# Scores of q from two products a half: agents' leading and residual parts side by side as columns

## The chip, the cores and the metric

The kernel runs on one core of a Trainium2 chip. The metric is the device time of one execution in microseconds; the median of three runs is compared. A profile of one further execution gives the trace.

## The reference

Inputs: q, k and v of 2 x 12480 x 128, agents of 2 x 49 x 128, all float32; w_in (128 x 2048) and w_out (2048 x 128) in float64.

```
def sm(a, b):
    s = scale * (a @ b.transpose(0, 2, 1))
    s = s - s.max(-1, keepdims=True)
    e = exp(s)
    return e / (e.sum(-1, keepdims=True) + 1e-9)
agent_v = sm(agents, k) @ v          # 49 x 128 per batch
x = sm(q, agents) @ agent_v          # 24960 tokens x 128
h = x @ w_in
out = maximum(0.01 * h, h) @ w_out
```

Attention through 49 agents, then two layers with a leaky ReLU on every token.

## The kernel before

**Blocks and steps.** The 24960 tokens go in 52 blocks of 480 (26 of each batch), channels first. A block has eight steps p. A step computes 2 x 128 of the 2048 hidden channels (`mm1`, which takes the attention's weights pT straight to hidden channels through a product of agent_v and w_in, in m_hi and m_lo), evicts them through ReLU as a leading part hi (ScalarE, line 702) and a residue lo (VectorE, line 703), and two steps later (LAG = 2) adds them into the output (`mm2`, line 719). Products run on rounded float32 (F32R), so every operand is split into a leading part and a residue, and each product is the sum of three. The linear part of the leaky ReLU is one more product of pT with l_hi and l_lo (line 729), added at p = 4.

**Halves.** In `mm1`, `mm2` and `q_mm` every product contracts over 64 partitions, the lower half (0 to 63) or the upper (64 to 127), and the two of a pair write different banks, g = 0 and g = 1. In `mm1` the halves hold two groups of hidden channels' weights, because pT has all 49 agents in each half; in `mm2` and `q_mm` they are the two parts of a sum, and somebody has to add the banks up. In `mm2` `o_copy` (ScalarE, line 740, one copy of both banks) and `o_add` (GpSimd) do that; the output tile has one buffer, so the first output product of a block waits for the copy of the block before. Program order is o_copy of block i - 1, then `mm1` of block i's step 2, then the side work of the step, then `mm2` of step 0.

**Slots.** The 49 agents stand in four groups of 32 columns (SLOTS): agents 0 to 24, 25 to 48, 25 to 48, 0 to 24, so that 32 x 32 transpositions on VectorE work on them.

**The chain of q.** For every block a chain of small operations makes pT, spread over the steps ahead of the block by the table `chain`: (-14, q_mm) means 14 steps before the block's first. q_hi (ScalarE) and q_lo (GpSimd) split q; q_mm makes the scores (six products, line 589); q_x (ScalarE, line 596) copies bank 1 and q_add (VectorE, line 602) adds bank 0; q_tr transposes; q_red takes a maximum over the agents of a slot; q_swap (GpSimd, lines 618 and 619) exchanges the halves' maxima; q_mx, q_sub, q_exp, q_sum, q_swap, q_rec, q_norm complete the softmax; p_trans transposes back; p_hi and p_lo split it. In a step the instructions are issued in the order `mm1`, ReLU, side work, `mm2`; each engine takes its own in that order. The bank pair of the scores (tag "x", one buffer) is shared with the key scores, the value sums and the weight products of batch 1.

**Around it.** Batch 0's keys, values, weights and its first chain come ahead of the loop, in an order that a planner makes from listed costs; the chain of block 1 is packed into steps 0 to 6 of block 0 (`early`). Batch 1's key scores run in blocks 0 to 6, its weighted values (`k_av2`) in blocks 9 to 21, its weights in 22 to 24.

```
    chain = (
        (-17, q_hi), (-17, q_lo), (-14, q_mm), (-14, q_x), (-14, q_add), (-13, q_tr),
        (-12, q_red), (-12, q_swap), (-11, q_mx), (-11, q_sub), (-9, q_exp), (-8, q_sum),
        (-8, q_swap), (-7, q_rec), (-7, q_norm), (-6, p_trans), (-4, p_hi), (-4, p_lo),
    )
```

Of the kernel before, what the change touches and what calls it, by code (L numbers as in the profile page):

```python
# [8 lines left out]
F32 = mybir.dt.float32  # L9
F32R = mybir.dt.float32r  # L10
# [3 lines left out]
ALU = mybir.AluOpType  # L14
# [49 lines left out]
def tile_agent_attention_then_leaky_mlp(  # L64
# [33 lines left out]
    NB = G * TP  # L100
# [38 lines left out]
    ps_o = ctx.enter_context(tc.tile_pool(name="ps_o", bufs=1, space=PSUM))  # L139
# [15 lines left out]
    w_out_sb = const.tile([P, NF, C], F32, tag="wm", name="w_out_sb")  # L155
    wo_hi = const.tile([P, NF, C], F32R, name="wo_hi")
    wo_lo = const.tile([P, NF, C], F32R, name="wo_lo")
    ww = const.tile([P, C], F32, name="ww")
    a_sb = const.tile([P, B, NA], F32, name="a_sb")
    a_hi = [const.tile([P, P], F32R, name=f"a_hi{b}") for b in range(B)]  # L160
    a_lo = [const.tile([P, P], F32R, name=f"a_lo{b}") for b in range(B)]
    m_hi = [const.tile([P, DFF], F32R, name="m_hi0"), None]
    m_lo = [const.tile([P, DFF], F32R, name=f"m_lo{b}") for b in range(B)]
    l_hi = [const.tile([P, C], F32R, name=f"l_hi{b}") for b in range(B)]
# [110 lines left out]
    wT = {}  # L275
# [15 lines left out]
    def ww_mm(n):  # L291
        for j in range(4):
            f = 4 * n + j
            nc.tensor.matmul(  # L294
                avw[0][:, 1, :C], lhsT=wT[n][:, j * P:(j + 1) * P], rhs=w_out_sb[:, f, :],
                start=False, stop=(f == NF - 1),
            )

    def ww_end():
        nc.scalar.mul(ww, avw[0][:, 1, :C], SLOPE)  # L300

    def scale(eng, o, x, f=1.0, add=0.0):
        if eng is nc.scalar:
# [6 lines left out]
    def sub(eng, o, x, y):  # L310
        eng.tensor_tensor(out=o, in0=x, in1=y, op=ALU.subtract)  # L311


    SLOTS = (0, 0, A0), (SL, A0, NA - A0), (2 * SL, A0, NA - A0), (3 * SL, 0, A0)

    def prep_a(b):
        a = a_sb[:, b, :]
        a_sl = p1.tile([P, P], F32, tag="avs", name="a_sl")
        nc.gpsimd.memset(a_sl, 0.0)
        for o, x, n in SLOTS:  # L320
            nc.vector.tensor_copy(a_sl[:, o:o + n], a[:, x:x + n])
        for o in (SL, 2 * SL):
            nc.vector.tensor_copy(a_sl[:, o + A0 - 1:o + A0], a[:, A0 - 1:A0])
        nc.vector.tensor_copy(a_hi[b], a_sl)
        sub(nc.vector, a_lo[b], a_sl, a_hi[b].bitcast(F32))
# [99 lines left out]
    av_t, avw = {}, []  # L425
# [21 lines left out]
    def av_zero(b, first):  # L447

        if first:
            av_t[b] = avw[0][:, 0, :C + 2]  # L450
        z = m_lo[1][:TP, :C + 2]
        nc.tensor.matmul(av_t[b], lhsT=z[:, :P], rhs=z, start=first, stop=not first)

# [115 lines left out]
    qs_t, s_t, x_t, r_t2, pT_t = {}, {}, {}, {}, {}  # L569
# [12 lines left out]
    def q_mm(i):  # L582
        b = i // BPB
        hi, lo = qs_t.pop(i)
        ps = aux2()
        for n, (w, x) in enumerate(((a_hi, hi), (a_lo, hi), (a_hi, lo))):
            for g in range(2):
                r = slice(g * HALF, (g + 1) * HALF)
                nc.tensor.matmul(  # L589
                    ps[:, g, :NB], lhsT=w[b][r], rhs=x[r], start=(n == 0), stop=(n == 2)  # L590
                )
        s_t[i] = ps

# [4 lines left out]

    def q_add(i):
        ps, x = s_t[i]  # L600
        s = p1.tile([P, NB], F32, tag="sq", name="sq")
        nc.vector.tensor_tensor(out=s, in0=ps[:, 0, :NB], in1=x, op=ALU.add)
        s_t[i] = s

    def q_tr(i):
# [9 lines left out]

    def q_swap(i):
        r = r_t2[i]
        nc.gpsimd.tensor_copy(r[:HALF, :, 1], r[HALF:, :, 0])  # L618
        nc.gpsimd.tensor_copy(r[HALF:, :, 1], r[:HALF, :, 0])

    def q_mx(i):
        r = r_t2.pop(i)
# [55 lines left out]
    h_t, r_t, o_t = {}, {}, {}  # L678
# [30 lines left out]
    def mm2(i, p):  # L709

        b = i // BPB
        if p == 0:
            o_t[i] = ps_o.tile([P, 2, MC], F32, tag="o", name="o")
        o = o_t[i]
        hi, lo = r_t.pop((i, p))

        def add(w, x, start=False, stop=False):
            for g, r in enumerate(ROWS):
                nc.tensor.matmul(o[:, g, :NB], lhsT=w[r], rhs=x[r], start=start, stop=stop)  # L719

        for g in range(2):
            f = 2 * p + g
            add(wo_hi[:, f, :], hi[:, g], start=(f == 0))
            add(wo_lo[:, f, :], hi[:, g])
        if p == NP // 2:
            t = pT_t[i]
            for w, x, g in ((l_hi, 0, 0), (l_lo, 0, 1), (l_hi, 1, 0)):
                r = ROWS[g]
                nc.tensor.matmul(  # L729
                    o[:, g, :NB], lhsT=w[b][r], rhs=t[r, x], start=False, stop=False  # L730
                )
        for g in range(2):
            f = 2 * p + g
            add(wo_hi[:, f, :], lo[:, g], stop=(f == NF - 1))

    def o_copy(i):
        t = p1.tile([P, 2, NB], F32, tag="oT", name="oT")
        o = o_t.pop(i)
        if i < NBLK - 1:
            nc.scalar.copy(t, o[:, :, :NB])  # L740
            x_t["o"] = t
            return
        h = NB // 2
        for c, eng in ((slice(0, h), nc.sync), (slice(h, NB), nc.scalar)):
            nc.scalar.copy(t[:, 1, c], o[:, 1, c])
            nc.vector.tensor_tensor(out=t[:, 0, c], in0=o[:, 0, c], in1=t[:, 1, c], op=ALU.add)
            eng.dma_start(out=out[:, i * NB + c.start:i * NB + c.stop], in_=t[:, 0, c])

    def o_add(i):
# [7 lines left out]
    def at(step, fn, *a):  # L757
        side.setdefault(step, []).append((fn, a))


    chain = (
        (-17, q_hi), (-17, q_lo), (-14, q_mm), (-14, q_x), (-14, q_add), (-13, q_tr),
        (-12, q_red), (-12, q_swap), (-11, q_mx), (-11, q_sub), (-9, q_exp), (-8, q_sum),
        (-8, q_swap), (-7, q_rec), (-7, q_norm), (-6, p_trans), (-4, p_hi), (-4, p_lo),
    )

    early = (0, 0, 0, 0, 1, 1, 2, 2, 3, 4, 4, 5, 5, 6, 6, 6)
    for i in range(1, NBLK):
        at(NP * i + LAG, o_add, i - 1)
    for r, (_, fn) in zip(early, chain[2:]):  # L770
# [8 lines left out]
    for b in range(1, B):  # L779
# [3 lines left out]
        for c in range(NCH):  # L783
            s = n0 + c // 2 * NP
# [33 lines left out]
        for m in range(0, NM, 2):  # L818
            s = n0 + 5 + (m // 2 + 1) * NP
# [5 lines left out]
    with tc.manual_schedule():  # L825
        nc.sync.dma_start(out=a_sb, in_=agents)
        loads = [(x, ORDER[:i].count(x)) for i, x in enumerate(ORDER)]
        warm = m_lo[1][:, :MC]
# [8 lines left out]
        for t in [pd] + er:  # L837
            nc.gpsimd.memset(t.bitcast(F32), 0.0)

        avw.append(ps_o.tile([P, 2, MC], F32, tag="o", name="avw"))  # L840

        def heat(n, start=False):

            for i in range(n if ("wmm", NM - 1) not in plan.done else 0):
                nc.tensor.matmul(
                    avw[0][:, 1, :], lhsT=warm[:, :P], rhs=warm, start=start and i == 0, stop=False
                )

        plan = Plan(HOP, {"pe": 6000, "dve": 6500, "act": 2500, "pool": 5000, "dma": 3000})
# [12 lines left out]
        dve, act = nc.vector, nc.scalar  # L862
# [24 lines left out]
        for n in range(2 * NM):  # L887
            r = [("mul", n - RP)] if n >= RP else []
            add(("bits", n), "dve", 940, conv_bits, (n,), [("w", n)] + r)
            add(("mant", n), "act", 620, conv_mant, (n, act), [("bits", n)])  # L890
            add(("exp", n), "act", 1440, conv_exp, (n,), [("bits", n)])
            add(("low", n), "dve", 620, conv_low, (n,), [("mant", n)])
            add(("sign", n), "dve", 680, conv_sign, (n,), [("exp", n)])
            add(("mul", n), "dve", 600, conv_mul, (n, dve), [("low", n), ("sign", n)])
            if n % 2:
                add(("wohi", n), "act", 620, wo_hi_of, (n, act), [("mul", n)])
            if n == 1:
                add(("wolo", n), "dve", 680, wo_lo_of, (n,), [("wohi", n)])
# [16 lines left out]
        for c in range(NCH):  # L915
# [91 lines left out]
```

## Time and profile before

| what | value |
|---|---|
| median of 3 runs | 981.24 us (981.02 to 981.54) |
| profiled execution | 980.12 us, its span 978.3 us |
| TensorE busy, mean granted clock | 961.8 us, 1.000 |
| VectorE, ScalarE, GpSimd busy | 727.1, 602.8, 385.6 us |

The span runs from the first to the last instruction; 1.8 us of the profiled execution lie around it. Busy times are shares of the span; TensorE overlaps products, so its busy time says that something was in flight, not how much.

### The profile page before, as it was taken

The page shows a single profiled execution, that of the slowest core. Times are in us where ns is not written, and L with a number is a line of the kernel's source. Part 1 is how long each engine was busy: PE and PEld are TensorE (multiplying, and loading weights), DVE is VectorE, ACT ScalarE, POOL GpSimd, SP SyncE. Part 2 cuts the span into 40 slices and gives each one's busy share as a digit, 9 for nine tenths or more (in the row PEclk, how much of TensorE's full clock was granted, in tenths as well). Part 3 has the DMA queues.
Part 4 walks back from the last instruction along what each step waited for, and adds up shares of the span by engine and source line. Part 5 has one row for each costly group of instructions (what it writes and reads, how often), then busy time and mean ns, then how long its engine had stood idle before and what let it go on. Part 6 is the DMA issues. An engine that isn't in the chain of part 4 may idle for free.

```text
span 978.3 us, 22378 instructions
## 1 busy us (share of the span) xinstructions
PE 961.8 (98%) x9336; PEld 824.4 (84%) x9336; DVE 727.1 (74%) x1071; ACT 602.8 (62%) x806; POOL 385.6 (39%) x557
## 2 busy tenths in 40 slices
PE   8889999999999999999999999999999999999998
PEld 6767888888888888888888888888888888888886
DVE  6967677778787787787776777777777777677764
ACT  5755565566666666665665666665666666666653
POOL 2113233346666556563443333333333333333320
PEclk9999999999999999999999999999999999999999
DMA  9931112112112122110010101101010101010000
GB/s 347 368 139 63 62 62 91 53 42 83 42 42 82 43 59 65 41 42 22 21 41 22 42 21 33 31 22 42 21 42 21 41 21 42 21 37 26 22 21 21
DMA packets 24032, 57.68 MB, mean 59 GB/s; under 512 B 2787, under 2 KB 16355, under 8 KB 23931
## 3 DMA queue, kind: packets, MB, share of 16 engines
q1 hardware_dynamic: 23787, 56.13, 17.5%
q8 instruction: 73, 1.20, 0.5%
q14 instruction: 28, 0.23, 0.1%
q10 hardware_dynamic: 144, 0.12, 0.0%
HBM read 43.46 MB, written 12.78 MB: 57 GB/s over the span
## 4 chain that ended last, share of the span: by engine, by line
PE 94%; DVE 2%; DMA 2%; issue 1%; ACT 1%; SPq 0%; POOL 0%; POOLq 0%; ACTq 0%
PE o L719 56%; PE h L689 26%; PE aux L589 4%; PE o L729 2%; PE aux L435 1%; PE aux L343 1%; DMA kt<-in_k_dram 1%; PE sc L343 1%; DMA vt<-in_v_dram 1%; PE avw L459 1%; DVE lo L703 1%; DVE run L354 0%; PE avw L294 0%; PE mp L525 0%; DVE w_out_sb L264 0%
## 5 line engine op out<-in xcount | busy, mean ns | idle before, releaser
L703 DVE SCALAR_TENSOR_TENSOR lo<-h,hi 128x960 fp32r<-128x960 f32 x416 | 481.3, 1157 | 220.5 <-ACT hi L702 214.1
L702 ACT ACTIVATE hi<-h 128x960 fp32r<-128x960 f32 x416 | 405.0, 974 | 312.0 <-PE h L689 306.6
L719 PE MATMUL o<-hi,wo_hi 64*128 64x480 f32 x1664 | 365.6, 383 | 0.8 <-ACT oT L740 0.8
L719 PE MATMUL o<-hi,wo_lo 64*128 64x480 f32 x1664 | 357.6, 376 | 0.0
L689 PE MATMUL h<-pT,m_hi 64*128 64x480 f32 x1664 | 293.0, 378 | 1.9 <-DVE lo L703 1.1
L719 PE MATMUL o<-lo,wo_hi 64*128 64x480 f32 x1664 | 291.8, 376 | 0.0
L719 PEld LDWEIGHTS o<-hi,wo_hi 64*128 64x128 f32 x1664 | 210.9, 184 | 32.7 <-ACT oT L740 9.7
L719 PEld LDWEIGHTS o<-hi,wo_lo 64*128 64x128 f32 x1664 | 211.8, 184 | 22.6
L689 PEld LDWEIGHTS h<-pT,m_hi 64*128 64x128 f32 x1664 | 193.4, 184 | 25.7 <-DVE lo L703 2.6
L719 PEld LDWEIGHTS o<-lo,wo_hi 64*128 64x128 f32 x1664 | 195.1, 184 | 22.7
L689 PE MATMUL h<-pT,m_lo 64*128 64x480 f32 x832 | 201.0, 376 | 0.0
L311 POOL TENSOR_TENSOR qlo<-qt,qhi 128x480 fp32r<-128x480 f32 x52 | 64.2, 1235 | 170.6 <-ACT qhi L573 170.6
L689 PEld LDWEIGHTS h<-pT,m_lo 64*128 64x128 f32 x832 | 114.9, 184 | 12.0
L311 POOL TENSOR_TENSOR pT<-pt,pT 128x480 fp32r<-128x480 f32 x52 | 63.7, 1225 | 139.9 <-ACT pT L670 139.9
L658 POOL TENSOR_TENSOR pd<-d,rs 128x375 f32<-128x375 f32 x52 | 42.8, 823 | 87.0 <-DVE rs L653 83.4
L751 POOL TENSOR_TENSOR oT<-oT 128x480 f32<-128x480 f32 x51 | 62.6, 1228 | 9.9 <-ACT oT L740 9.9
L311 POOL TENSOR_TENSOR d<-st,mm 128x375 f32<-128x375 f32 x52 | 43.7, 841 | 48.8 <-DVE mm L624 47.6
L740 ACT COPY oT<-o 128x960 f32<-128x960 f32 x51 | 49.1, 962 | 16.1 <-PE o L719 16.1
L618 POOL COPY sm<-sm 64x15 f32<-64x15 f32 x52 | 10.2, 196 | 78.0 <-DVE sm L638 76.1
L311 POOL TENSOR_TENSOR vr<-vt,vr 120x512 fp32r<-120x512 f32 x26 | 33.9, 1303 | 13.4 <-DVE vr L306 13.4
L665 DVE STREAM_TRANSPOSE pt<-pd 128x480 f32<-128x480 f32 x52 | 34.8, 670 | 0.0
L607 DVE STREAM_TRANSPOSE st<-sq 128x480 f32<-128x480 f32 x52 | 34.7, 667 | 0.0
(130 smaller groups left out, 862.0 us busy)
## 6 DMA issues: line engine op xcount, KB each, us to landing
qt<-in_q_dram SPq DMA_DIRECT2D x53, 240.0 KB, 2.8
kt<-in_k_dram SPq DMA_DIRECT2D x26, 480.0 KB, 7.6
out_dram<-oT SPq DMA_DIRECT2D x51, 240.0 KB, 2.0
vt<-in_v_dram SPq DMA_DIRECT2D x13, 520.0 KB, 7.8
vt<-in_v_dram SPq DMA_DIRECT2D x13, 487.5 KB, 4.8
w<-in_w_in_dram SPq DMA_DIRECT2D x4, 512.0 KB, 6.8
w<-in_w_out_dram SPq DMA_DIRECT2D x4, 512.0 KB, 7.6
out_dram<-oT SPq DMA_DIRECT2D x1, 120.0 KB, 1.7
```

What stands on the lines that cost most here:

```text
L311: eng.tensor_tensor(out=o, in0=x, in1=y, op=ALU.subtract)
L343: nc.tensor.matmul(ps[r, j * NA:(j + 1) * NA], lhsT=k_t[b, c][:, j, r], rhs=a_sb[:, b, :], start=True, stop=True,)
L589: nc.tensor.matmul(ps[:, g, :NB], lhsT=w[b][r], rhs=x[r], start=(n == 0), stop=(n == 2))
L607: nc.vector.transpose(t.rearrange("p n a -> p (n a)"), s_t[i])
L658: nc.gpsimd.tensor_tensor(out=pd[:, :, :A0], in0=d, in1=w.to_broadcast([P, NT, A0]), op=ALU.mult,)
L665: nc.vector.transpose(t, pd.rearrange("p n a -> p (n a)"))
L689: nc.tensor.matmul(ps[:, g, :NB], lhsT=w[b][r, cols(2 * p + g)], rhs=t[r, x], start=(n == 0), stop=(n == 2),)
L702: nc.scalar.activation(hi, ps, AF.Relu)
L703: nc.vector.scalar_tensor_tensor(out=lo, in0=ps, scalar=0.0, in1=hi.bitcast(F32), op0=ALU.max, op1=ALU.subtract,)
L719: nc.tensor.matmul(o[:, g, :NB], lhsT=w[r], rhs=x[r], start=start, stop=stop)
L740: nc.scalar.copy(t, o[:, :, :NB])
L751: nc.gpsimd.tensor_tensor(out=t[:, 0], in0=t[:, 0], in1=t[:, 1], op=ALU.add)
```

## The change

The agents' leading parts take columns 0 to 63 of a weight tile a_w and their residues columns 64 to 127, so that one product of a half gives both: leading parts of q with both parts of the agents, then the residue of q with both (which adds the product of the two residues). That is four products a block in place of six. The result's two halves of partitions now have to be added: q_add puts the sum of the banks back into bank 0, `q_cross` copies each half of the partitions over to the other half (ScalarE, two copies), and `q_add2` adds them. The slots are 0 to 24, 25 to 48, 0 to 24, 25 to 48, so `q_swap` exchanges neighbouring groups of 32 partitions in four copies in place of two of 64. Every later step of the chain comes one step later. The output's banks become two tiles, o0 and o1, with a copy each, and the odd product of the linear part changes sides from block to block.

```diff
-        a_sl = p1.tile([P, P], F32, tag="avs", name="a_sl")
+        a_sl = p1.tile([P, HALF], F32, tag="avs", name="a_sl")
...
+        nc.vector.tensor_copy(a_w[b][:, :HALF], a_sl)
+        sub(nc.vector, a_w[b][:, HALF:], a_sl, a_w[b][:, :HALF].bitcast(F32))
...
-        for n, (w, x) in enumerate(((a_hi, hi), (a_lo, hi), (a_hi, lo))):
+        for n, x in enumerate((hi, lo)):
             for g in range(2):
                 r = slice(g * HALF, (g + 1) * HALF)
                 nc.tensor.matmul(
-                    ps[:, g, :NB], lhsT=w[b][r], rhs=x[r], start=(n == 0), stop=(n == 2)
+                    ps[:, g, :NB], lhsT=a_w[b][r], rhs=x[r], start=(n == 0), stop=(n == 1)
                 )
...
     def q_add(i):
         ps, x = s_t[i]
+        ps = ps[:, 0, :NB]
+        nc.vector.tensor_tensor(out=ps, in0=ps, in1=x, op=ALU.add)
+        s_t[i] = ps
+
+    def q_cross(i):
+        ps = s_t[i]
+        x = p1.tile([P, NB], F32, tag="sx", name="sy")
+        nc.scalar.copy(x[:HALF], ps[HALF:])
+        nc.scalar.copy(x[HALF:], ps[:HALF])
+        s_t[i] = ps, x
+
+    def q_add2(i):
+        ps, x = s_t[i]
         s = p1.tile([P, NB], F32, tag="sq", name="sq")
-        nc.vector.tensor_tensor(out=s, in0=ps[:, 0, :NB], in1=x, op=ALU.add)
+        nc.vector.tensor_tensor(out=s, in0=ps, in1=x, op=ALU.add)
...
-        nc.gpsimd.tensor_copy(r[:HALF, :, 1], r[HALF:, :, 0])
-        nc.gpsimd.tensor_copy(r[HALF:, :, 1], r[:HALF, :, 0])
+        for o in range(0, P, SL):
+            x = o ^ SL
+            nc.gpsimd.tensor_copy(r[o:o + SL, :, 1], r[x:x + SL, :, 0])
...
-            o_t[i] = ps_o.tile([P, 2, MC], F32, tag="o", name="o")
+            o_t[i] = halves("o")
...
             for w, x, g in ((l_hi, 0, 0), (l_lo, 0, 1), (l_hi, 1, 0)):
+                g ^= i % 2 == 0
                 r = ROWS[g]
...
-            nc.scalar.copy(t, o[:, :, :NB])
+            for g in range(2):
+                nc.scalar.copy(t[:, g], o[g][:, :NB])
...
-        (-17, q_hi), (-17, q_lo), (-14, q_mm), (-14, q_x), (-14, q_add), (-13, q_tr),
-        (-12, q_red), (-12, q_swap), (-11, q_mx), (-11, q_sub), (-9, q_exp), (-8, q_sum),
-        (-8, q_swap), (-7, q_rec), (-7, q_norm), (-6, p_trans), (-4, p_hi), (-4, p_lo),
+        (-17, q_hi), (-17, q_lo), (-14, q_mm), (-14, q_x), (-14, q_add), (-13, q_cross),
+        (-13, q_add2), (-12, q_tr), (-11, q_red), (-11, q_swap), (-10, q_mx), (-10, q_sub),
+        (-8, q_exp), (-7, q_sum), (-7, q_swap), (-6, q_rec), (-6, q_norm), (-5, p_trans),
+        (-3, p_hi), (-3, p_lo),
...
-    early = (0, 0, 0, 0, 1, 1, 2, 2, 3, 4, 4, 5, 5, 6, 6, 6)
+    early = (0, 0, 0, 0, 0, 1, 1, 1, 2, 2, 3, 4, 4, 5, 5, 6, 6, 6)
```

`halves` makes one tile of one bank for each g. The planner's list gets the two new operations and their costs, and batch 0's use of the output banks ahead of the loop moves to the two tiles.

## Rows read from the trace of the kernel before

**Rows 1.** The page: busy time by engine; the chain that ended last.

```profile
PE 961.8 (98%) x9336; PEld 824.4 (84%) x9336; DVE 727.1 (74%) x1071; ACT 602.8 (62%) x806; POOL 385.6 (39%) x557
...
PE 94%; DVE 2%; DMA 2%; issue 1%; ACT 1%; SPq 0%; POOL 0%; POOLq 0%; ACTq 0%
```

**Rows 2.** Groups of instructions by line: count, busy us, mean ns.

```profile
L729 PE MATMUL o<-pT,l_hi 64*128 64x480 f32 x104 | 30.7, 375 | 0.0
L589 PE MATMUL aux<-qhi,a_lo 64*128 64x480 f32 x104 | 29.5, 373 | 0.0
L729 PE MATMUL o<-pT,l_lo 64*128 64x480 f32 x52 | 19.5, 376 | 0.0
```

**Rows 3.** Timeline of TensorE: start, duration, line, tiles; first products of steps.

```profile
709.32 0.60 PE L689 MATMUL h<-pT,m_hi 64*128 64x480 f32 x4
711.27 0.60 PE L689 MATMUL h<-pT,m_hi 64*128 64x480 f32 x4
715.19 0.60 PE L689 MATMUL h<-pT,m_hi 64*128 64x480 f32 x4
```

**Rows 4.** The chain that ended last, in order of time: start, duration.

```profile
133.34 2.00 PE aux L343 x61
152.35 2.00 PE aux L343 x62
808.80 1.33 PE o L719 x11
825.58 1.33 PE o L719 x11
```

**Rows 5.** Timeline of TensorE at a block's linear part.

```profile
716.73 0.38 PE L729 MATMUL o<-pT,l_lo 64*128 64x480 f32 x1
716.94 0.37 PE L729 MATMUL o<-pT,l_hi 64*128 64x480 f32 x1
716.95 0.81 PE L719 MATMUL o<-lo,wo_hi 64*128 64x480 f32 x4
```

**Rows 6.** Timeline of all engines from one block's output to the next's.

```profile
706.05 0.80 PE L719 MATMUL o<-lo,wo_hi 64*128 64x480 f32 x4
706.89 0.96 ACT L740 COPY oT<-o 128x960 f32<-128x960 f32 x1 [0.34 <-PE o L719]
707.75 0.98 ACT L702 ACTIVATE hi<-h 128x960 fp32r<-128x960 f32 x1
707.91 0.19 PEld L719 LDWEIGHTS o<-hi,wo_hi 64*128 64x128 f32 x2 [0.16 <-ACT oT L740]
708.01 0.19 PEld L719 LDWEIGHTS o<-hi,wo_lo 64*128 64x128 f32 x2
```

**Rows 7.** Waits of the weight loads: us in total, times, longest.

```profile
PEld o L719 <- ACT oT L740: 9.7, 51, 0.9
PEld h L689 <- DVE lo L703: 2.6, 4, 1.1
```

**Rows 8.** Timeline of all engines in the first steps of block 0.

```profile
65.29 0.56 ACT L596 COPY sx<-aux 128x480 f32<-128x480 f32 x1
65.74 0.59 ACT L573 CAST qhi<-qt 128x480 fp32r<-128x480 f32 x1
66.23 0.98 ACT L702 ACTIVATE hi<-h 128x960 fp32r<-128x960 f32 x1
66.45 0.65 DVE L602 TENSOR_TENSOR sq<-aux,sx 128x480 f32<-128x480 f32 x1
68.30 1.15 DVE L703 SCALAR_TENSOR_TENSOR lo<-h,hi 128x960 fp32r<-128x960 f32 x1
```

**Rows 9.** Timeline of GpSimd and VectorE in a quiet block.

```profile
706.36 0.20 POOL L618 COPY sm<-sm 64x15 f32<-64x15 f32 x1 [1.52 <-DVE sm L638]
711.19 1.16 DVE L703 SCALAR_TENSOR_TENSOR lo<-h,hi 128x960 fp32r<-128x960 f32 x1
712.26 0.67 DVE L607 STREAM_TRANSPOSE st<-sq 128x480 f32<-128x480 f32 x1
713.13 1.16 DVE L703 SCALAR_TENSOR_TENSOR lo<-h,hi 128x960 fp32r<-128x960 f32 x1 [0.20 <-ACT hi L702]
```

More of the change, by code (lines that the diff above doesn't have):

```diff
@@ L146, in aux, with halves @@
         return aux2()[:, 0, :]
+    def halves(name):
+        return [ps_o.tile([P, MC], F32, tag=f"o{g}", name=f"{name}{g}") for g in range(2)]
     def pair(name):
@@ L159, in tile_agent_attention_then_leaky_mlp @@
     a_sb = const.tile([P, B, NA], F32, name="a_sb")
-    a_hi = [const.tile([P, P], F32R, name=f"a_hi{b}") for b in range(B)]
-    a_lo = [const.tile([P, P], F32R, name=f"a_lo{b}") for b in range(B)]
+    a_w = [const.tile([P, P], F32R, name=f"a_w{b}") for b in range(B)]
     m_hi = [const.tile([P, DFF], F32R, name="m_hi0"), None]
@@ L294, in ww_mm @@
             nc.tensor.matmul(
-                avw[0][:, 1, :C], lhsT=wT[n][:, j * P:(j + 1) * P], rhs=w_out_sb[:, f, :],
+                avw[1][:, :C], lhsT=wT[n][:, j * P:(j + 1) * P], rhs=w_out_sb[:, f, :],
                 start=False, stop=(f == NF - 1),
@@ L299, in ww_end @@
     def ww_end():
-        nc.scalar.mul(ww, avw[0][:, 1, :C], SLOPE)
+        nc.scalar.mul(ww, avw[1][:, :C], SLOPE)
     def scale(eng, o, x, f=1.0, add=0.0):
@@ L311, in sub @@
         eng.tensor_tensor(out=o, in0=x, in1=y, op=ALU.subtract)
-    SLOTS = (0, 0, A0), (SL, A0, NA - A0), (2 * SL, A0, NA - A0), (3 * SL, 0, A0)
+    SLOTS = (0, 0, A0), (SL, A0, NA - A0), (2 * SL, 0, A0), (3 * SL, A0, NA - A0)
     def prep_a(b):
         a = a_sb[:, b, :]
-        a_sl = p1.tile([P, P], F32, tag="avs", name="a_sl")
+        a_sl = p1.tile([P, HALF], F32, tag="avs", name="a_sl")
         nc.gpsimd.memset(a_sl, 0.0)
-        for o, x, n in SLOTS:
+        for o, x, n in SLOTS[:2]:
             nc.vector.tensor_copy(a_sl[:, o:o + n], a[:, x:x + n])
[L322 to L325, printed above, removed]
+        nc.vector.tensor_copy(a_sl[:, SL + A0 - 1:SL + A0], a[:, A0 - 1:A0])
+        nc.vector.tensor_copy(a_w[b][:, :HALF], a_sl)
+        sub(nc.vector, a_w[b][:, HALF:], a_sl, a_w[b][:, :HALF].bitcast(F32))
     sc_t, sc_pair, mb = {}, {}, {}
@@ L449, in av_zero @@
         if first:
-            av_t[b] = avw[0][:, 0, :C + 2]
+            av_t[b] = avw[0][:, :C + 2]
         z = m_lo[1][:TP, :C + 2]
@@ L718, in add @@
             for g, r in enumerate(ROWS):
-                nc.tensor.matmul(o[:, g, :NB], lhsT=w[r], rhs=x[r], start=start, stop=stop)
+                nc.tensor.matmul(o[g][:, :NB], lhsT=w[r], rhs=x[r], start=start, stop=stop)
         for g in range(2):
@@ L727, in mm2 @@
             for w, x, g in ((l_hi, 0, 0), (l_lo, 0, 1), (l_hi, 1, 0)):
+                g ^= i % 2 == 0
                 r = ROWS[g]
                 nc.tensor.matmul(
-                    o[:, g, :NB], lhsT=w[b][r], rhs=t[r, x], start=False, stop=False
+                    o[g][:, :NB], lhsT=w[b][r], rhs=t[r, x], start=False, stop=False
                 )
@@ L744, in o_copy @@
         for c, eng in ((slice(0, h), nc.sync), (slice(h, NB), nc.scalar)):
-            nc.scalar.copy(t[:, 1, c], o[:, 1, c])
-            nc.vector.tensor_tensor(out=t[:, 0, c], in0=o[:, 0, c], in1=t[:, 1, c], op=ALU.add)
+            nc.scalar.copy(t[:, 1, c], o[1][:, c])
+            nc.vector.tensor_tensor(out=t[:, 0, c], in0=o[0][:, c], in1=t[:, 1, c], op=ALU.add)
             eng.dma_start(out=out[:, i * NB + c.start:i * NB + c.stop], in_=t[:, 0, c])
@@ L838, in tile_agent_attention_then_leaky_mlp @@
             nc.gpsimd.memset(t.bitcast(F32), 0.0)
-        avw.append(ps_o.tile([P, 2, MC], F32, tag="o", name="avw"))
+        avw.extend(halves("avw"))
         def heat(n, start=False):
@@ L845, in heat @@
                 nc.tensor.matmul(
-                    avw[0][:, 1, :], lhsT=warm[:, :P], rhs=warm, start=start and i == 0, stop=False
+                    avw[1], lhsT=warm[:, :P], rhs=warm, start=start and i == 0, stop=False
                 )
@@ L900, in tile_agent_attention_then_leaky_mlp @@
                 m = n // 2
-                old = [("wcopy", m - 1)] if m else [("chain", 4)]
+                old = [("wcopy", m - 1)] if m else [("chain", 6)]
                 old += [("mm", 0), f_rec] * (m >= NM - 2)
@@ L925, in tile_agent_attention_then_leaky_mlp @@
             q_hi: ("act", 493), q_lo: ("pool", 1158), q_mm: ("pe", 403), q_x: ("act", 451),
-            q_add: ("dve", 569), q_tr: ("dve", 569), q_red: ("dve", 459), q_swap: ("pool", 340),
+            q_add: ("dve", 569), q_cross: ("act", 1100), q_add2: ("dve", 569), q_tr: ("dve", 569), q_red: ("dve", 459), q_swap: ("pool", 680),
             q_mx: ("dve", 84), q_sub: ("pool", 773), q_exp: ("act", 406), q_sum: ("dve", 444),
```

## The prediction

> **What bounds the kernel now.** I read the page first. TensorE is busy through 98% of the span at the full granted clock, and the chain that ended last lies on it for 94% [rows 1]. So the first question is what one product costs there, and the second what makes it wait.
>
> The groups of lines name the products that the change touches [rows 2]: the scores of q take three groups of 104 on line 589 (one is shown), six products a block of q and three pairs, each half of the partitions having one of a pair. The linear part takes three on line 729, two of them (104 and 52 by block) in the lower half, one in the upper.
>
> The TensorE timeline gives the beat. Steps without extras hold nine pairs each; one starts at 709.32, the next at 711.27 and the third behind that at 715.19 [rows 3]: 5.87 us for 27 pairs, 0.2175 a pair. A product is recorded as 0.38 us long, but a half of the partitions takes a new one every beat. A quiet block is 16.78 us long (its pattern recurs at 808.80 and 825.58) [rows 4]. It holds 72 products per half in the two layers, 3 for the scores, and 2 in the lower half but 1 in the upper for the linear part: 77 and 76. 77 beats are 16.75 us, which leaves 0.03. So the lower half alone sets the block, and the upper idles a beat in it.
>
> Where does the upper half idle? At the linear part the third product is lower, and the first product behind it in the program is lower too. Yet line 719 has a start 0.01 us from the third one's [rows 5]. One half cannot stream two products at once, so I read this as the upper half's product having gone ahead of an earlier lower one. The upper half is then a beat ahead until the next block's output bank: there its first output product waits for the copy of the bank [rows 6].
>
> The table of waits says that this wait costs the weight loads 9.7 us in 51 blocks, and that waits for the residue of the first layer (lo) cost 2.6 us in four places [rows 7]. Nothing else holds TensorE up in the main loop.
>
> **The change, part by part.**
>
> Products. Each half loses one score product a block (77 becomes 76, 76 becomes 75), and the extra linear product is lower in odd blocks, upper in even ones. Over two blocks a half has 2 x 74 + 3 = 151 products, 75.5 a block: 75.5 x 0.2175 = 16.42 us, 0.35 less than 16.78. That is only had if the lead of one half over the other survives the output bank.
>
> Output bank. Let T be the last output product's start, 706.05 + 0.80 - 0.38 = 706.47 [rows 6]. The copy starts at T+0.42 (706.89), takes 0.96, frees ScalarE for the next after 0.86 (707.75), and the weight load follows 0.05 behind its end (707.91); weights take 0.10 more (the next load is at 708.01). The lower half, due seven beats behind T (T+1.52 = 707.99), loses 0.02. After the change it is due at six beats, T+1.31. A copy of one bank of 480 takes 0.57 us with 0.45 from it to the next on ScalarE (65.29 to 65.74) [rows 8]. If both halves end together: first bank released at T+0.42+0.57+0.05 = T+1.04, in time; second copied from T+0.87 to T+1.44, streaming from T+1.59, so the upper half is 0.28 late, and the next lower product, behind it in the queue, about as much less a beat. From then on the lower half is a beat ahead, and its bank ends a beat before T: copies from T+0.20 and T+0.66, second streaming at T+1.38, 0.07 late. If it is two beats ahead (behind an even block's linear part) the second copy can start at T+0.42 and nothing is late. So a steady pair of blocks pays about 0.08, a block 0.04. Bounds: nothing, if the copies go faster; 0.45 a block, if the copies start together and the second waits for the end of the first (0.42 + 2 x 0.57 + 2 x 0.05 + 0.10 = 1.76 against 1.31). I take 0.04, since the ScalarE rows overlap.
>
> Per quiet block: 16.78 - 16.42 - 0.04 = 0.31 us gained. By the program, 41 of 52 blocks use TensorE by halves only (batch 1's value products also have 64 rows a half): 12.7 us.
>
> The seven blocks with key scores (19.01 us each, 133.34 to 152.35) [rows 4] are different: those are full-height products, both halves must meet ahead of them. An even block keeps 76 beats (gain near 0.16), an odd one pays the 0.28 at the bank and the meeting (loss near 0.06): 0.4 us together. The four blocks that make batch 1's weights: 0.2 each, 0.8.
>
> The work added elsewhere. ScalarE gets two copies over half the partitions for q_cross, which I price like a whole one (0.45 each), and about 0.06 from the split copy. VectorE gets q_add2, 0.65 like q_add [rows 8]. GpSimd gets four swap copies more a block at 0.20 [rows 9]. All are hidden if the first layer's residue is in time. The tightest place is the residue of a block's fifth step, on VectorE from 713.13 to 714.29; TensorE needs its bank two steps later, at 715.19: 0.90 to spare [rows 3, 9]. In the new order VectorE has there, behind the previous residue (from 711.19, its follower at 712.26), p_trans, a transposition like the 0.67 one that stands there now, and q_add2; each starts about 0.08 before its forerunner has ended, as 712.26 does. The residue then starts at 712.26 + 0.59 + 0.57 = 713.42, or up to 0.2 later where the one before is later, 0.3 to 0.5 behind its old place, and TensorE comes 0.1 to 0.3 earlier, so 0.1 to 0.5 remains. The value stage, with a cast more in front, is where it would go first. q_cross itself queues on ScalarE behind the fourth step's activation and ends about when the next one is ready. GpSimd's sum over the output now goes ahead of q_norm, for which VectorE's p_trans waits, but p_trans stands a step later too. I take nothing; if the cover is gone, each 0.1 us costs 4 to 5 us over the loop.
>
> The head. Block 1's chain is squeezed into block 0, where step 0 now holds q_mm to q_add2 at once. q_add ended at 66.45 + 0.65 = 67.10; q_cross waits for it on ScalarE, ahead of the second activation, which now starts at 66.23 and would at about 68.05 [rows 8]. Its residue (68.30 before) moves to about 69.05, and the next ones wait for q_add2 and the moved transposition: 1 to 2.5 us, I take 1.7. Block 0's own chain grows by a copy pair and an addition among the conversions of the weights, against cheaper agents' parts: 0 to 1, I take 0.5. Both are lost once.
>
> Sum: 12.7 + 0.4 + 0.8 - 1.7 - 0.5 = 11.7 us gained, from the profiled 980.12 (span 978.3 and 1.8 around it): 968.4; the median of the runs is 1.1 higher, 981.24, so 969.5.
>
> **Rivals.**
>
> Strict order between the halves. If the lower half cannot run two beats ahead, an even block's linear part stops it for one beat, both end together behind an odd one, and the bank costs 0.28 in one block of two and 0.07 in the other. A block is then 16.42 + 0.18 = 16.60 and the gain 0.18 at most, 0.15 with the weight loads of the stopped half: 41 x 0.15 + 0.9 - 2.2 = 4.9, so 976. For it: running two ahead has the lower half start a product behind a waiting upper one, which no row shows in that direction. Against it: rows 5 show the upper half doing the same. The Trainium skill's page "TensorE: Matmul & The Clock Gate" (Part 3, The mechanism) says that matmuls start and end strictly in program order. By that rule this rival is right and the gain near 5 us; by rows 5 the order between halves is loose and it is near 12.
>
> The second bank is the new wait, and it ends slower. The upper half's first output product waits for a second copy that starts only when the first is done, and the wait blocks the queue for both halves. It is a loss from 0.35 us a block on, where it eats the 1.5 beats; at the bound of 0.45 a block is 16.87, 0.10 longer: 41 x 0.10 and 2.2 at the head, 987.5. For it: the bank is already the one wait of the loop [rows 7]. Against it: ScalarE's rows start before the one ahead has ended [rows 6, 8].
>
> Late residues. VectorE or GpSimd are some 0.2 us a block later than I worked out: 41 x 0.11 + 1.2 - 2.2 = 3.5, so 977.7, or no gain at 0.3. For it: the 0.1 to 0.5 left is the least in the loop. Against it: waits of this kind are four in the whole run [rows 7].
>
> **How the numbers follow.** Forecast 0.50, strict order 0.22, late residues 0.14, second bank 0.14. A change under 0.2% (2 us) is about what a measurement of this kernel cannot tell from none. Faster: 0.50, 0.21 of strict order and 0.08 of late residues: 0.79. Same: 0.08, from late residues and a mild second bank. Slower: 0.13, nearly all second bank. The forecast's own range is 966 (no late bank, 0.35 x 41, a head that costs 1) to 974. For 8 in 10 I go up to 978.5, through strict order and the better part of late residues, and leave out the rest of it and the slower rival.
>
> **What will show it.** Right: quiet blocks at 16.4 to 16.5 us on average; two starts on line 589 per half and block; weight loads' wait for the output copies at 0 to 0.1 us a block; ScalarE's two output copies 0.45 apart, the first starting before the upper half's last product is out; block 0 one or two us longer. Strict order: blocks near 16.6, and linear parts of even blocks with a lone product. Second bank: 0.4 us of wait on line 719's loads in every block. Late residues: waits of line 689's loads for lo in every block. I am wrong altogether if the beat itself changes, 0.2175 being the unit of every term.

## The result, and the profile after

The changed kernel takes 994.04 us (median of 4 runs, 993.39 to 995.18) against 981.2: a ratio of 1.0132 (95% interval 1.0114 to 1.0149), 12.8 us slower, where 969.5 was forecast. (Two of the ten executions of x1_oadd_late, the profiled one among them, ran at a granted clock of 0.56 throughout; its time is the median of the other eight, and no time is read from its profile.)

The page of the changed kernel, for [rows 1]:

```profile
span 991.5 us, 22510 instructions
...
PE 968.8 (98%) x9233; PEld 844.8 (85%) x9233; DVE 789.7 (80%) x1117; ACT 664.4 (67%) x961; POOL 430.1 (43%) x765
...
PE 87%; DVE 5%; ACT 3%; issue 2%; DMA 2%; POOL 0%; SPq 0%; DVEq 0%; ACTq 0%; POOLq 0%
```

TensorE is as "busy" as before, but the chain that ended last leaves it for 13% of the time, most of that for VectorE and ScalarE. Its groups of lines (one for [rows 2], and two that the argument needs now):

```profile
L592 PE MATMUL aux<-qhi,a_w 64*128 64x480 f32 x104 | 31.0, 381 | 1.6 <-DVE sq L618 1.6
...
L663 DVE SCALAR_TENSOR_TENSOR rs<-sm 128x15 f32<-128x15 f32 x52 | 38.1, 733 | 0.0
...
L310 DVE CAST vr<-vt 120x512 fp32r<-120x512 f32 x26 | 24.1, 929 | 0.0
```

The scores' products are two groups of 104 now. The row to stop at is line 663, the first instruction of q_rec: 15 elements per partition, 733 ns on average, 166 before.

The waits of the weight loads, for [rows 7]:

```profile
PEld h L706 <- DVE lo L720: 15.5, 42, 1.3
PEld o L736 <- ACT oT L759: 11.8, 53, 0.4
```

The wait for the output's copies is still there (9.7 before), and the residue, late in 4 places before, is late in 42.

Where the span's 13.1 us went, from the starts of the blocks' first products in the two traces (a block from its first `mm1` product to the next block's):

| stretch | before | after | difference |
|---|---|---|---|
| up to block 0's first product | 63.4 | 64.6 | +1.2 |
| block 0 | 19.4 | 23.0 | +3.6 |
| block 1 | 20.0 | 20.4 | +0.4 |
| blocks 2 to 6 (key scores) | 94.1 | 94.0 | -0.1 |
| block 7 | 17.3 | 19.3 | +2.0 |
| blocks 8 to 20 (value stage) | 230.4 | 236.1 | +5.7 |
| blocks 21 to 24 | 73.4 | 75.0 | +1.5 |
| blocks 25 to 50 (quiet) | 436.2 | 435.5 | -0.7 |
| block 51 and the end | 24.2 | 23.5 | -0.7 |

The quiet blocks, in which 0.31 us each had been forecast, gained 0.03. Blocks 0, 7 and 8 to 24 lost most. The first row is no loss of the change that these traces show: the kernels of x2_before_collide and x11_before_two_pairs start block 0 at 64.3 and 65.9 us, later than the one before by 0.9 and 2.5.

VectorE and GpSimd in a quiet block of the changed kernel, for [rows 9]:

```profile
739.63 1.16 DVE L720 SCALAR_TENSOR_TENSOR lo<-h,hi 128x960 fp32r<-128x960 f32 x1 [0.43 <-ACT hi L719]
740.71 0.86 DVE L663 SCALAR_TENSOR_TENSOR rs<-sm 128x15 f32<-128x15 f32 x1
741.61 0.19 DVE L667 TENSOR_TENSOR rs<-rs,d 128x15 f32<-128x15 f32 x1
...
744.20 0.62 DVE L618 TENSOR_TENSOR sq<-aux,sy 128x480 f32<-128x480 f32 x1
744.82 1.16 DVE L720 SCALAR_TENSOR_TENSOR lo<-h,hi 128x960 fp32r<-128x960 f32 x1
```

```profile
740.04 0.19 POOL L636 COPY sm<-sm 32x15 f32<-32x15 f32 x1
740.31 1.23 POOL L770 TENSOR_TENSOR oT<-oT 128x480 f32<-128x480 f32 x1
742.16 0.83 POOL L675 TENSOR_TENSOR pd<-d,rs 128x375 f32<-128x375 f32 x1 [0.62 <-DVE rs L670]
```

q_rec's instruction starts at 740.71, stands for 0.86 and ends at 741.57; GpSimd's o_add ran from 740.31 to 741.54. Of the 52 instances 50 end 0.03 us behind such a GpSimd instruction (48 behind o_add, two behind a subtraction for batch 1's weights), and the two that meet none take 0.15 and 0.16. GpSimd's own queue is not the delay: q_norm (742.16) waited for VectorE, with GpSimd idle for 0.62 us ahead of it. All later work of VectorE in the block is late by this: the residue of the fifth step starts at 744.82 and ends at 745.98, and TensorE goes on at 746.04 where it was due at 745.86:

```profile
745.43 0.79 PE L736 MATMUL o<-lo,wo_hi 64*128 64x480 f32 x4
746.04 0.70 PE L706 MATMUL h<-pT,m_hi 64*128 64x480 f32 x4
746.58 0.38 PE L706 MATMUL h<-pT,m_lo 64*128 64x480 f32 x2
```

The four products from 746.04 take 0.54 to the next line, where they take 0.43 without a wait: the load of the weights is exposed as well.

### The profile page after: what moved, and what is told of

The parts are those of the page before. It is cut to its first block, busy times and chain, and to the rows that moved or that the text cites. A ratio compares the mean times of both kernels' runs of the same rounds, so it can differ in the third digit from the quotient of the medians.

```text
span 991.5 us, 22510 instructions
## 1 busy us (share of the span) xinstructions
PE 968.8 (98%) x9233; PEld 844.8 (85%) x9233; DVE 789.7 (80%) x1117; ACT 664.4 (67%) x961; POOL 430.1 (43%) x765
## 4 chain that ended last, share of the span: by engine, by line
PE 87%; DVE 5%; ACT 3%; issue 2%; DMA 2%; POOL 0%; SPq 0%; DVEq 0%; ACTq 0%; POOLq 0%
PE o L736 52%; PE h L706 26%; PE aux L592 2%; PE o L747 2%; PE aux L438 1%; ACT hi L719 1%; PE aux L346 1%; DVE lo L720 1%; PE sc L346 1%; DMA vt<-in_v_dram 1%; ACT oT L759 1%; DVE rs L663 1%; DMA w<-in_w_out_dram 1%; PE avw L462 1%; DVE aux L605 1%
## 5 line engine op out<-in xcount | busy, mean ns | idle before, releaser
L736 PE MATMUL o<-hi,wo_hi 64*128 64x480 f32 x1664 | 419.9, 383 | 0.0
L736 PE MATMUL o<-hi,wo_lo 64*128 64x480 f32 x1664 | 415.4, 379 | 0.0
L706 PE MATMUL h<-pT,m_hi 64*128 64x480 f32 x1664 | 333.8, 384 | 3.3 <-DVE lo L720 1.6
L736 PE MATMUL o<-lo,wo_hi 64*128 64x480 f32 x1664 | 333.8, 376 | 0.0
L736 PEld LDWEIGHTS o<-hi,wo_hi 64*128 64x128 f32 x1664 | 270.1, 184 | 30.8 <-ACT oT L759 11.8
L736 PEld LDWEIGHTS o<-hi,wo_lo 64*128 64x128 f32 x1664 | 270.2, 184 | 17.1
L736 PEld LDWEIGHTS o<-lo,wo_hi 64*128 64x128 f32 x1664 | 233.6, 185 | 17.1
L706 PE MATMUL h<-pT,m_lo 64*128 64x480 f32 x832 | 236.1, 376 | 0.0
L636 POOL COPY sm<-sm 32x15 f32<-32x15 f32 x208 | 40.1, 193 | 194.9 <-DVE sm L655 188.4
L636 POOL COPY mx<-mx 32x15 f32<-32x15 f32 x208 | 41.3, 199 | 49.7 <-DVE mx L629 42.5
L759 ACT COPY oT<-o 128x480 f32<-128x480 f32 x102 | 52.1, 563 | 11.2 <-PE o L736 8.4
```

The costliest lines, as they stand in the source:

```text
L636: nc.gpsimd.tensor_copy(r[o:o + SL, :, 1], r[x:x + SL, :, 0])
L706: nc.tensor.matmul(ps[:, g, :NB], lhsT=w[b][r, cols(2 * p + g)], rhs=t[r, x], start=(n == 0), stop=(n == 2),)
L736: nc.tensor.matmul(o[g][:, :NB], lhsT=w[r], rhs=x[r], start=start, stop=stop)
L759: nc.scalar.copy(t[:, g], o[g][:, :NB])
```

## The experiments

Three questions: is VectorE late by the meeting with GpSimd (theory P) or by its own added work (V); what became of the score pair's beat at the output bank (theory B); what made block 0 and block 7 long.

**1. x1_oadd_late.** The changed kernel with:

```diff
-        at(NP * i + LAG, o_add, i - 1)
+        at(NP * i + LAG + 2, o_add, i - 1)
```

> The changed kernel with the sum over the output (o_add on GpSimd) issued two steps later, in a block's step 4 in place of step 2; nothing else. Theory P (port): q_rec's first instruction on VectorE, which reads two SBUF operands, waits until o_add on GpSimd has ended (mean 733 ns against 166 before), and this lateness reaches the residue that TensorE waits for. Then its mean falls to about 165 ns, quiet blocks from 16.76 to 16.45 to 16.6 us, blocks of the value stage from 18.2 to about 17.6, the whole from 994 to about 981. Rival V (work): VectorE is late because q_add2 and the order of the chain give it more to do at that place, whoever runs on GpSimd. Then blocks and time stay (993 to 995).

Measured: 980.38 us (ratio to before 0.9993, 0.9983 to 1.0003). The edit of one number takes 13.7 us off the changed kernel (994.04 - 980.38), all that it had lost; the rest is within the interval. Lengths are read from x4_oadd_early below, which has the same edit: line 663 takes 0.16 to 0.18 us in 50 of 52 blocks (0.65 in two, beside a subtraction for batch 1's weights), quiet blocks 16.39 and 16.83 us in turn, those of the value stage 17.69 (18.22 before the edit). P holds. Every second quiet block, though, is as long as before the change.

**2. x2_before_collide.** The kernel before with

```diff
-        (-8, q_swap), (-7, q_rec), (-7, q_norm), (-6, p_trans), (-4, p_hi), (-4, p_lo),
+        (-8, q_swap), (-6, q_rec), (-6, q_norm), (-5, p_trans), (-3, p_hi), (-3, p_lo),
```

> The kernel before with q_rec and q_norm one step later, p_trans, p_hi and p_lo one step later, so that q_rec stands behind o_add as in the changed kernel; products, banks and the rest are those of before. Theory P: the first instruction of q_rec goes from 166 ns to 650 to 900 in nearly every block, and the time rises by 0 to 4 us over 981, since the residue of the fifth step had 0.9 us to spare. Rival V: 166 ns and 981 stay.

Measured: 981.26 us (1.0004, 0.9994 to 1.0014), 165 ns. The two never met: with the sum and its two swap copies left where they were, o_add starts earlier than in the changed kernel and has ended when q_rec comes. The run speaks for neither theory; it shows that this part of the chain may come a step later at no cost. It shows one thing more: the cast of v in the value stage is held by GpSimd here (0.73 us on average, 0.41 before), and blocks 9 to 20 still take 213.27 us (213.37 before).

**3. x5_before_four_swaps** is the mended form: the kernel before with q_exp to p_lo a step later, and four swap copies.

```diff
-        nc.gpsimd.tensor_copy(r[:HALF, :, 1], r[HALF:, :, 0])
-        nc.gpsimd.tensor_copy(r[HALF:, :, 1], r[:HALF, :, 0])
+        for o in range(0, P, SL):
+            x = o ^ HALF
+            nc.gpsimd.tensor_copy(r[o:o + SL, :, 1], r[x:x + SL, :, 0])
```

> The kernel before with GpSimd's side of the change alone: the softmax's tail (q_exp to p_lo) one step later and each swap in four copies of 32 partitions in place of two of 64, so that o_add starts later and q_rec meets it; products, banks and additions are those of before. Theory P (q_rec waits for o_add on GpSimd): q_rec's first instruction goes from 166 ns to 550 to 800 in most blocks; the time rises by 0 to 1 us at most, since the residue has 0.9 us to spare here. Theory V (VectorE late by its own work): 166 ns.

Measured: 988.56 us (1.0078, 1.0063 to 1.0093), more than either theory said. VectorE and GpSimd in a block of its value stage:

```profile
313.23 1.16 DVE L704 SCALAR_TENSOR_TENSOR lo<-h,hi 128x960 fp32r<-128x960 f32 x1 [0.58 <-ACT hi L703]
314.30 0.70 DVE L647 SCALAR_TENSOR_TENSOR rs<-sm 128x15 f32<-128x15 f32 x1
...
315.94 0.76 DVE L306 CAST vr<-vt 120x512 fp32r<-120x512 f32 x1
```

```profile
313.75 1.22 POOL L752 TENSOR_TENSOR oT<-oT 128x480 f32<-128x480 f32 x1
315.59 0.82 POOL L659 TENSOR_TENSOR pd<-d,rs 128x375 f32<-128x375 f32 x1 [0.62 <-DVE rs L654]
```

The instruction has 702 ns on average here too, without a product, a bank or an addition of the change. Quiet blocks stay at 16.78, as expected; blocks 9 to 20 take 218.92 us in place of 213.37. There the cast of v stands behind q_rec and meets q_norm (0.76 in this block, 0.64 on average, against 0.41), and TensorE's weight loads wait for the residue 22 times in 200 us. The cast alone is not enough: it is held as long in x2_before_collide (213.27 us) and longer in x4_oadd_early (0.96 on average, 212.28 us), where q_rec is not. So a loss of the size of the value stage's in the changed kernel (213.37 to 218.67) comes with GpSimd's side of the change alone. (The edit also moves q_exp and q_sum a step later; no run has that by itself.)

**4. x6_one_copy.** Run 1 with the output in one tile and one copy again:

```diff
-        return [ps_o.tile([P, MC], F32, tag=f"o{g}", name=f"{name}{g}") for g in range(2)]
+        whole.append(ps_o.tile([P, 2, MC], F32, tag="o", name=name))
+        return [whole[-1][:, g, :] for g in range(2)]
...
-            for g in range(2):
-                nc.scalar.copy(t[:, g], o[g][:, :NB])
+            nc.scalar.copy(t, whole[-1][:, :, :NB])
```

> The changed kernel with o_add two steps later, and the output in one tile of two banks with one copy again (the linear product still changes sides). Theory B (bank): with a score pair less, the next block's first output product is due 1.31 us behind the last one's start, and one copy frees the banks for streaming only at 1.54, so a quiet block is 76 beats and 0.23, 16.76 us, as before the change, and the whole is 985 to 988. Rival: the split is worth nothing, quiet blocks stay at the mean of 16.61 (two blocks of 16.39 and 16.83) and the whole at 980.5.

Measured: 985.64 us (1.0048, 1.0033 to 1.0063), quiet blocks 16.77. As B said.

**5. x11_before_two_pairs.** The kernel before with one score pair less, whose product is left out; nothing else.

```diff
-        for n, (w, x) in enumerate(((a_hi, hi), (a_lo, hi), (a_hi, lo))):
+        for n, (w, x) in enumerate(((a_hi, hi), (a_hi, lo))):
```

> The kernel before with two score pairs a block in place of three: the product of q's leading part with the agents' residue is left out. One tile, one copy, chain and swaps of before, so none of the change's costs are in it. Theory B (bank): the copy of the output banks is done 1.54 us behind the last output product's start and the shorter step comes to it at 1.31, so quiet blocks stay at 16.76 to 16.78 us and the whole within 1.5 of 981. Rival: the pair is worth its beat, 16.56 in quiet blocks and 970 to 972.

Measured: 980.62 us (0.9997, 0.9989 to 1.0006), quiet blocks 16.77. All engines from one block's output to the next's in this run:

```profile
708.38 0.80 PE L719 MATMUL o<-lo,wo_hi 64*128 64x480 f32 x4
...
709.22 0.96 ACT L740 COPY oT<-o 128x960 f32<-128x960 f32 x1 [0.34 <-PE o L719]
...
709.67 0.59 PE L589 MATMUL aux<-qlo,a_hi 64*128 64x480 f32 x2
...
710.23 0.19 PEld L719 LDWEIGHTS o<-hi,wo_hi 64*128 64x128 f32 x2 [0.38 <-ACT oT L740]
```

T is 708.80. In the kernel before, where T is 706.47, the last score products are these:

```profile
707.56 0.59 PE L589 MATMUL aux<-qlo,a_hi 64*128 64x480 f32 x2
```

They start a beat sooner in run 5 (T+0.87 against T+1.09), the copy does not, and the load that waits for it is at T+1.43, as before (707.91 - 706.47 = 1.44). The wait of 0.16 has become 0.38. The pair of products that the change takes out was worth nothing in the kernel as it stood.

**6. x7_split_only.** The kernel before with two output tiles, a copy each, and the alternating linear product:

```diff
+                g ^= i % 2 == 0
...
-            nc.scalar.copy(t, o[:, :, :NB])
+            for g in range(2):
+                nc.scalar.copy(t[:, g], o[g][:, :NB])
```

> The kernel before with the other part of the change alone: output in two tiles with a copy each, and the odd linear product changing sides. Scores, chain and swaps are those of before. By the lanes: 76.5 beats and at most 0.04 of waiting, 16.65 to 16.69 us in quiet blocks, and the whole 976 to 978. Rival (halves in strict order, one beat lost where the lead would be two): 16.72 to 16.78 and 979 to 981.

Measured: 975.77 us (0.9947, 0.993 to 0.9963), quiet blocks 16.55 and 16.76 in turn, mean 16.65: 76.5 beats. This part of the change alone beats both kernels.

**7. x12_split_two_pairs.** The same with the product of run 5 left out.

> The run x7_split_only with the same product left out: two tiles with a copy each, sides of the linear product changing, two score pairs, and none of the change's further work. Theory B: by the bank's two copies and the lost lead, quiet blocks at 16.39 and 16.83 in turn (mean 16.61) as in x8_head, against 16.65 of x7; the whole 973 to 975.5. Rival: without q_cross, q_add2 and the later chain the beat comes back, mean 16.44 and 968 to 970.

Measured: 973.68 us (0.9926, 0.9912 to 0.9939), quiet blocks 16.41 and 16.81, mean 16.60. None of the change's further work is in this run, so that work is not what costs the beat. With the split, the score pair is worth 2.1 us in all, where its beat over 52 blocks would be 11.3.

**8. x3_early and x4_oadd_early.** Block 1's chain spread wider over block 0, on the changed kernel and on run 1:

```diff
-    early = (0, 0, 0, 0, 0, 1, 1, 1, 2, 2, 3, 4, 4, 5, 5, 6, 6, 6)
+    early = (0, 0, 0, 1, 1, 2, 2, 2, 3, 3, 4, 5, 5, 5, 5, 6, 6, 6)
```

> The changed kernel with block 1's chain spread wider over block 0: q_cross and q_add2 in step 1 in place of 0, the transposition and its followers in step 2, and so on. If ScalarE's wait for q_add ahead of the second activation made block 0 long (23.0 us against 19.4, with a stretch at half the clock), block 0 falls to 19.5 to 21 us and the time by 2 to 3.5. Rival: VectorE's additional work in block 0 makes it long; then less than 0.7.

> Both edits of the two runs on the changed kernel, o_add two steps later and block 1's chain spread wider. By theory P with the head's: 977 to 979, below the kernel before. By V: 991.

Measured: 994.74 us (1.0138, 1.0122 to 1.0155) and 981.59 us (1.001, 0.9997 to 1.0024), both above what was expected. Block 0 became longer, not shorter: 23.6 and 24.9 us. So taking q_cross from ahead of the second activation does not help. TensorE in block 0 of the changed kernel shows another wait:

```profile
67.82 0.70 PE L706 MATMUL h<-pT,m_hi 64*128 64x480 f32 x4 [0.91 <-DVE lo L720]
68.36 0.38 PE L706 MATMUL h<-pT,m_lo 64*128 64x480 f32 x2
70.33 0.49 PE L592 MATMUL aux<-qhi,a_w 64*128 64x480 f32 x2 [1.58 <-DVE sq L618]
71.90 0.49 PE L592 MATMUL aux<-qlo,a_w 64*128 64x480 f32 x2 [1.08 <-POOL qlo L315]
```

Block 2's scores wait for the bank that block 1's scores hold until q_add2 (line 618), 1.58 us; in both runs above the same wait is 2.29. The clock that was granted then:

```profile
68.00:72.00 4.00, 1.34 (x10) 0.63 (x10) 2.58 (x4) 3.43 (x5) 1.66 (x1) 1.00 0.00 0
72.00:76.00 4.00, 4.00 (x24) 3.37 (x26) 3.97 (x8) 1.00 (x2) 1.94 (x5) 0.60 0.00 0
```

(By stretch: busy time of TensorE, its weight loads, VectorE, ScalarE and GpSimd, then the granted clock.) TensorE is busy for 1.34 of 4 us, and in the next 4 us the clock is 0.60 on average, most of it at half, 1.2 GHz. With 0.97 in the 4 us behind those, that is an estimated 1.7 us of work at the full clock (4 x 0.40 + 4 x 0.03) out of the 3.6 that block 0 lost. In x4_oadd_early the clock is 0.86, 0.50 and 0.79 in the three stretches of 4 us from 66 to 78.

**9. x8_head.** The kernel of x4_oadd_early with the two places mended where TensorE waits for that bank: the chain of block 2 from q_mm to p_trans, and k_max2 and k_max3 in block 7, a step later.

```diff
-            at(max(NP * n + r, 0), fn, n)
+            at(max(NP * n + r + (n == 2 and -14 <= r <= -5), 0), fn, n)
...
-        for p, fn in ((1, k_max0), (3, k_max1), (3, k_max1d), (7, k_max2), (7, k_max3)):
+        for p, fn in ((1, k_max0), (3, k_max1), (3, k_max1d), (8, k_max2), (8, k_max3)):
```

> The changed kernel with o_add two steps later and the places mended where TensorE waited for the bank of the scores, which is now held until q_add2: in block 0 the chain of block 1 spread wider and that of block 2 a step later; in block 7 the product of the key maxima (k_max2) a step later. If that bank made block 0 23 to 25 us long and block 7 19.3, they fall to 20 to 21 and 17.3, and the whole to 974 to 977. Rival: they are long by VectorE's and ScalarE's work, and the whole stays at 979 to 981.

Measured: 978.39 us (0.9973, 0.9962 to 0.9984), above the 974 to 977 expected. Block 7 falls from 19.0 to 17.3, as expected; block 0 only from 24.9 to 23.3, because now its key scores wait for the same bank:

```profile
78.11 0.34 PE L346 MATMUL aux<-a_sb,kt 128*64 128x49 f32 x2 [2.46 <-DVE sq L618]
```

**10. x9_lower_first.** Run 9 with another order of a block's first products, both of the lower half ahead of the upper's:

```diff
+            if f == 0:
+                for n, r in enumerate(ROWS):
+                    nc.tensor.matmul(o[n][:, :NB], lhsT=wo_hi[r, f, :], rhs=hi[r, g], start=True, stop=False)
+                    nc.tensor.matmul(o[n][:, :NB], lhsT=wo_lo[r, f, :], rhs=hi[r, g], start=False, stop=False)
+                continue
```

> The run x8_head with another order of a block's first four output products: both of the lower half (wo_hi, wo_lo), then both of the upper, in place of taking turns. Theory Q (queue): behind an even block the lower half is two beats ahead, but its second output product stands in the queue behind the upper half's first, which waits for the second bank's copy, so the lead falls to one and an odd block is 77.3 beats. Then odd blocks fall from 16.82 to 16.50 to 16.65 us, even ones stay within 0.1 of 16.41, and the whole falls from 978.4 to 973 to 975.5. Rival: the lead is lost for another reason (the weights' load or the copy itself); then 16.82 stays and the whole is 978.

Measured: 975.42 us (0.9943, 0.9931 to 0.9956). Quiet blocks are 16.31 and 16.70 in turn, mean 16.50 (x8: 16.61). The sum of two blocks fell by 0.22 as Q wants, but even ones gained nearly as much as odd ones, so the account by parity was not right, though the time is within what it expected.

**11. x10_block0.** Run 10 with block 2's q_cross and q_add2 back in step 3.

> The run x9_lower_first with block 2's q_cross and q_add2 back in step 3 (its q_mm stays in step 3), so that the key scores of block 0 in step 5 find the bank free sooner. If the bank of the scores is what makes block 0 long (23.3 us), it falls to 20.5 to 22 and the whole by 1 to 3 more; rival: ScalarE's and VectorE's queues in block 0 are full either way, and it stays within 0.7.

Measured: 975.55 us (0.9953, 0.994 to 0.9967); block 0 is 23.1, block 1 21.6 (20.0 in x9). No gain. Its trace shows what stands in place of the shorter wait: block 0's key scores wait less for the bank (1.57 us, 2.44 in x9), and the granted clock stays at 1.00 up to 86 us; but block 1's first product, with which block 0 ends, waits 1.78 us for ScalarE's cast of pT (line 687), and the stretch at half the clock now falls into block 1 (0.65 from 86 to 90 us). Whether block 0 would come back to 19.4 with the bank free and block 1's pT in time was not reached by any run and stays open.

## Why the prediction was wrong

**The step that failed first** is the one on GpSimd: "GpSimd's sum over the output now goes ahead of q_norm ... I take nothing". I looked at the order of GpSimd's queue and not at what runs on VectorE beside it. Two shifts that I had each costed at nothing (q_sum and its swap a step later, two more copies in that swap) put o_add beside q_rec, whose first instruction reads two SBUF operands and waits until o_add has ended: 733 ns against 166. That is 0.57 us of VectorE a block, at a place where the forecast left 0.1 to 0.5 us of cover. Runs 1 and 3 show it from both sides: without the meeting the changed kernel is 13.7 us faster, and the kernel before with the meeting is 7.6 slower (988.56 - 980.92). The rival "late residues" had the mechanism (TensorE waits for lo) but neither this cause nor its size in the value stage, where the blocks became 0.44 us longer than before and not shorter. The Trainium skill's page "SBUF — State Buffer" (Who interferes with whom) says that a VectorE instruction with two SBUF inputs contends with a GpSimd instruction that reads SBUF, that the shared ports are an exclusive lock, and that issue order decides who blocks. The trace agrees: o_add started first (740.31 against 740.71), and 50 of 52 end 0.03 us behind the GpSimd instruction, at lengths of 0.64 to 0.96 by how early they came.

**The step that failed for good** is the output bank: a quiet block gained 0.17 us without the meeting (16.78 to 16.61 in x4), where 0.31 was forecast with 0.04 for the bank. The first half of that working was right to the last digit: in x4, between aligned halves, the copies, the first product and the load that waits for the second bank come at T+0.42, T+1.31 and T+1.49 (T = 711.74 + 0.59 - 0.38 = 711.95):

```profile
711.74 0.59 PE L736 MATMUL o<-lo,wo_hi 64*128 64x480 f32 x4
...
712.37 1.02 ACT L759 COPY oT<-o 128x480 f32<-128x480 f32 x2 [0.33 <-PE o L736]
...
713.26 0.67 PE L736 MATMUL o<-hi,wo_hi 64*128 64x480 f32 x2
...
713.44 0.18 PEld L736 LDWEIGHTS o<-hi,wo_hi 64*128 64x128 f32 x1 [0.21 <-ACT oT L759]
```

Then came "if it is two beats ahead the second copy can start at T+0.42 and nothing is late". The next block of the same run:

```profile
728.37 0.58 PE L736 MATMUL o<-lo,wo_hi 64*128 64x480 f32 x2
...
728.78 0.37 PE L736 MATMUL o<-lo,wo_hi 64*128 64x480 f32 x1
...
728.99 1.02 ACT L759 COPY oT<-o 128x480 f32<-128x480 f32 x2
...
729.45 0.38 PE L592 MATMUL aux<-qlo,a_w 64*128 64x480 f32 x1
729.60 0.18 PEld L736 LDWEIGHTS o<-hi,wo_hi 64*128 64x128 f32 x1
729.65 0.37 PE L592 MATMUL aux<-qhi,a_w 64*128 64x480 f32 x1
...
730.06 0.18 PEld L736 LDWEIGHTS o<-hi,wo_hi 64*128 64x128 f32 x1 [0.22 <-ACT oT L759]
730.06 0.29 PEld L736 LDWEIGHTS o<-hi,wo_lo 64*128 64x128 f32 x2
```

The lower half is two beats ahead: its second score product (729.45) starts before the upper's first (729.65). But the copies start at T+0.21 (T = 728.78), as for a lead of one, so the second bank comes late; the lower half's second output product (wo_lo, loads at 730.06) stands in the queue behind the load that waits for it, and the lead is gone. A pair of blocks is 16.39 + 16.83, mean 16.61: the number of the rival "strict order" (16.60), though the lower half did run two ahead. How the lead is lost is read from this pair of blocks and not shown by a run: run 10, which takes this order of products away, gained 0.10 us in the other blocks too and only 0.11 in these. The Trainium skill's page "TensorE: Matmul & The Clock Gate" (Part 3, The mechanism) says that matmuls start and end strictly in program order. These rows contradict it for starts (729.45 ahead of 729.65); for ends, as far as a copy's start tells of them, they agree: the copy of the lower bank begins 0.42 us behind the upper half's last product but one (728.57, the second of the two from 728.37) and not behind the lower half's own last (728.37).

Beneath it lies the larger miss: I priced the score pair at its beat, 0.2175 us. By run 5 it was worth nothing, since the products of the scores cover the copy of the bank; by runs 6 and 7 it is worth 0.04 a block with the split. The terms for other blocks were too large as well: with the meeting gone (x4), blocks 21 to 24 take 73.4 us as before, where 0.8 was forecast, and blocks 2 to 6 gain 0.2 together; the 19.01 us that the prediction gives for all seven blocks with key scores stand for blocks 2 to 5 alone. Of the 7.3 us of run 7, 5.2 are the split's and the alternation's, which need no change to the scores.

**A step that was missing**: the scores' bank pair, which batch 1's products and the next scores share, is now held until q_add2. It cost 2.0 us in block 7, where one product of the key maxima waits 1.7 for q_add2 (run 9 mends as much), and part of block 0's 3.6, with a stretch at half the clock behind it; how large a part stays open. The forecast had 2.2 for the whole head; blocks 0 and 1 alone lost 4.0.

What held: the beat (9.01 beats for a step of nine pairs in every profile at the full clock), the half beat a block that the alternating product gives (76.5 beats in run 6, from 77), the halves' ability to run ahead, and the first-order timing at the bank.

## What to carry to other kernels

A product that TensorE issues while it waits for something else anyway can be free, as here (980.62 us without it, 980.97 with it): before costing one away, find what ends last behind it, and try the removal alone (here one product left out). When a step moves in time, list for each of its instructions what runs beside it on the other of VectorE and GpSimd, operand by operand, not only what stands ahead of it in its queue. And take a change of several parts apart: here the split output banks gave 5.2 us, and the rest of the change on top of them cost 18.3 (994.0 - 975.8).

## What the runs showed of the hardware

A VectorE instruction of 0.17 us on two SBUF operands stood for up to 0.96 us beside a GpSimd addition and ended 0.03 us behind it; the cast of v (0.41 us before, 0.93 on average after) was held beside q_norm and k_sub and ended 0.28 us behind them in 25 of 26 cases. ScalarE's two copies to other partitions did not overlap: 0.57 from one start to the other (68.37 and 68.94 in block 0) against 0.46 for the output's (1.02 for two of 0.56). Products of the two halves of partitions started up to two beats out of program order.
